# A softmax without maxima, with its sums judged on the chip and a branch to a second version

## Chip, core and metric

One core of one Trainium2 chip runs the whole program. The metric is the device time of one execution in microseconds (us). Before the change three runs took 253.1, 253.52 and 254.39 us, median 253.52 us. The times of the parts below come from one further execution, recorded by the hardware profiler.

## What is computed

Grouped attention feeds a gated layer. There are 8 batches, 16 query heads, 4 key/value heads, 384 positions, head size 64. Cut to what matters:

```python
scores = q @ k.T / 8                       # per batch and head, 384 x 384
scores = scores - scores.max(-1)
attn = exp(scores);  attn = attn / (attn.sum(-1) + 1e-9)
x = (attn @ v)                             # 8 x 384 x 1024 after joining the heads
h = relu(x @ w_in);  u, v = h[:512], h[512:]
v_n = (v - mean(v)) / sqrt(var(v) + 1e-6)
v_s = w_spatial @ v_n + b_spatial          # mixes positions
out = (u * v_s) @ w_out                    # 8 x 384 x 1024, float32
```

The inputs q, k and v are normal draws times 0.1.

## The kernel before

The five engines are TensorE (PE; its weight loads are shown as PEld), VectorE (DVE), ScalarE (ACT), GpSimd (POOL) and SyncE (SP, which only issues DMAs). Each runs its own stream of instructions and waits for the others by semaphores. The order within every stream is the order in which the Python code emits instructions (`manual_schedule`), so a line's place in the code is its place in its engine's queue.

**Attention.** A batch is 18 steps of `scores` (L224): two matmuls give 128 keys by 1024 queries, and ACT takes the exponential (L240) straight from PSUM with a scale and no maximum. `weigh` (L242) multiplies the exponentials with v, to which a column of ones is appended, so that the sum of the exponentials comes out beside the weighted values. DVE then takes the reciprocal of four sums (L257) into a small tile `r` and scales the values with it (L259). There are 96 such calls, 12 for each batch.

**The gated layer.** `stream` (L424) is a generator that emits the gated layer's matmuls one after another: `v_tile` (L288), `u_block` (L358), `gate` (L375), `project` (L395). The main loop (L594) draws from it between the attention's steps, so that PE has matmuls while ACT works on exponentials. Inside `u_block`, at its fourth matmul, `normal` (L311) is emitted: ACT makes the reciprocal deviation, DVE the term `nmr` (L316), and POOL three times a normalised tile `vn` (L322). `gate` multiplies `vn` (L380), DVE adds the bias (L390), and the product with u (L392) goes to POOL, in the last batch alternately to POOL and DVE. `project` multiplies with w_out (L406), copies out of PSUM on DVE or ACT (L415) and lets SP issue the output DMA, in the last batch one for each piece (L419).

**The end.** After the last batch's attention nothing is left but the rest of the generator (L615): the last `v_tile`s, `u_block`s, `gate`s and `project`s. Then the launch code (L641) drains every engine, lets SP wait for the output DMAs, and joins the engines.

Of the kernel before, what the change touches and what calls it, by code (L numbers as in the profile page):

```python
# [17 lines left out]
def kernel(  # L18
# [59 lines left out]
    def load_k(b, eng=nc.sync):  # L78
        eng.dma_start(stage_tile("k", b), rows_of(k[b]))

    def load_v(b, eng=nc.sync):
        eng.dma_start(stage_tile("v", b), rows_of(v[b]))

    def load_q(b, j, eng=nc.sync):
        eng.dma_start(stage_tile("q", b, j), rows_of(q[b, 8 * j : 8 * j + 8]))
# [63 lines left out]
    def cast_k(b, eng, js=(0, 1)):  # L149
        if b not in k16s:  # L150
            k16s[b] = ld.tile([P, 2, NT, 2, D], FP16, name=f"k16_{b}", tag="k16")
        src = stage["k", b].rearrange("p (j h) (t d) -> p j h t d", h=2, t=NT)
        for hh in range(2):
            eng.tensor_copy(
                k16s[b][:, js[0] : js[-1] + 1, :, hh, :], src[:, js[0] : js[-1] + 1, hh]
            )

    def cast_v(b, eng):
        eng.tensor_copy(
            v1[b % 2][:, :, :, 0:D].rearrange("p g t d -> p (g t) d"),  # L160
            stage["v", b].rearrange("p g (t d) -> p (g t) d", t=NT),
        )

    def cast_q(b, j, eng, lo=0, hi=NT, other=None):
        if (b, j) not in q16s:
            q16s[b, j] = ld.tile([P, NT, G, 2, D], FP16, name=f"q16_{b}_{j}", tag="q16", bufs=4)
        src = stage["q", b, j].rearrange("p (h i) (t d) -> p h t i d", h=2, t=NT)
        for hh in range(2):
            f = other if hh and other else eng.tensor_copy
            f(q16s[b, j][:, lo:hi, :, hh, :], src[:, hh, lo:hi])  # L170
# [14 lines left out]
    def k_transposes(b, j, eng):  # L185
        ps = ps_ck.tile([P, S], FP16, name=f"kps_{b}_{j}", tag="ck")
        for t in range(NT):
            nc.tensor.transpose(
                ps[:, t * P : (t + 1) * P],
                k16s[b][:, j, t].rearrange("p h d -> p (h d)"),  # L190
                ident16,
            )
        eng(k_tile(b)[:, j], ps)

    def q_transposes(b, j, t, *engs):
        w = G // len(engs)
        for x, eng in enumerate(engs):
            ps = ps_ck.tile([P, w * P], FP16, name=f"qps_{b}_{j}_{t}_{x}", tag="ck")
            for i in range(w):
                nc.tensor.transpose(  # L200
                    ps[:, i * P : (i + 1) * P],
                    q16s[b, j][:, t, x * w + i].rearrange("p h d -> p (h d)"),
                    ident16,
                )
            eng(q_tile(b, j)[:, t, x * w * P : (x + 1) * w * P], ps)
# [13 lines left out]
        )  # L219


    aTs, avs, x16s, xts = {}, {}, {}, {}

    def scores(n):  # L224
# [17 lines left out]
    def weigh(b, m, hh):  # L242
        qt, j = divmod(m, 2)
        av = ps_av.tile([P, G, D + 1], FP32, name=f"av_{b}_{m}_{hh}", tag="av")
        for i in range(G):
            for t in range(NT):
                nc.tensor.matmul(  # L247
                    av[:, i, :],
                    aTs[b, m][:, t, hh, i * P : (i + 1) * P],
                    v1[b % 2][:, 2 * j + hh, t, 0 : D + 1],  # L250
                    start=(t == 0),
                    stop=(t == NT - 1),
                )
        if m == 0 and hh == 0:
            x16s[b] = att.tile([P, NT, NB, P], FP16, name=f"x16_{b}", tag="x16")
        r = small.tile([P, G, 1], FP32, name=f"r_{b}_{m}_{hh}", tag="r")
        nc.vector.reciprocal(r, av[:, :, D : D + 1])  # L257
        blk = 4 * j + 2 * hh
        nc.vector.tensor_tensor(  # L259
            x16s[b][:, qt, blk : blk + 2].rearrange("p k (i d) -> p (k i) d", i=2),  # L260
            av[:, :, 0:D],
            r.to_broadcast([P, G, D]),
            ALU.mult,
        )
# [13 lines left out]
    def x_turn(b, qt, lo, hi):  # L278
        nc.sync.dma_start(
            x_tile(b)[:, qt, lo:hi],  # L280
            x16s[b][:, qt, lo:hi].rearrange("p k s -> p (k s)"),
            transpose=True,
        )


    mvs, v_rs, v_ns, uTs, gTs, osbs = {}, {}, {}, {}, {}, {}
# [24 lines left out]
    def normal(b):  # L311
        rstd = small.tile([P, NT], FP32, name=f"rstd_{b}", tag="rstd")
        nmr = small.tile([P, NT], FP32, name=f"nmr_{b}", tag="nmr")
        nc.scalar.activation(rstd, mvs[b][:, :, 1], AF.Ln, bias=eps_t)
        nc.scalar.activation(rstd, rstd, AF.Exp, scale=-0.5)
        nc.vector.scalar_tensor_tensor(  # L316
            nmr, mvs[b][:, :, 0], -1.0, rstd, op0=ALU.mult, op1=ALU.mult
        )
        v_ns[b] = []
        for st in range(NT):  # L320
            vn = moe.tile([P, DH], FP16, name=f"vn_{b}_{st}", tag="vn", bufs=6)
            nc.gpsimd.tensor_scalar(  # L322
                vn,
                v_rs[b][st],
                rstd[:, st : st + 1],
                nmr[:, st : st + 1],
                op0=ALU.mult,
                op1=ALU.add,
            )
            v_ns[b].append(vn)  # L330
# [27 lines left out]
    def u_block(b, m):  # L358
        pu = ps_ck.tile([P, 512], FP32, name=f"pu_{b}_{m}", tag="ck")
        for kt in range(NB):  # L360
            nc.tensor.matmul(  # L361
                pu[:, 0:S].rearrange("p (t s) -> p t s", t=NT),
                w_in16[:, kt, m * P : (m + 1) * P],
                x_tile(b)[:, :, kt],
                start=(kt == 0),
                stop=(kt == NB - 1),
            )
            if m == 0 and kt == 3:
                normal(b)
            if kt < NB - 1:  # L370
                yield S
        nc.scalar.activation(uT_tile(b)[:, m, :], pu[:, 0:S], AF.Relu)
        yield S
# [21 lines left out]
    def project(b, tt, half):  # L395
        last = b == B - 1
        rows = out[b].rearrange("(p t) d -> p t d", t=NT)
        if half == 0:
            osbs[b, tt] = ops.tile([P, DM], FP32, name=f"osb_{b}_{tt}", tag="osb")
        osb = osbs[b, tt]  # L400

        cuts = (512, 768, 1024) if last and tt == NT - 1 and half else (512 * half, 512 * half + 512)
        for i, (lo, hi) in enumerate(zip(cuts, cuts[1:])):
            po = ps_ck.tile([P, 512], FP32, name=f"po_{b}_{tt}_{half}_{i}", tag="ck")
            for m in range(NM):
                nc.tensor.matmul(  # L406
                    po[:, 0 : hi - lo],
                    gTs[b][:, m, tt * P : (tt + 1) * P],
                    w_out16[:, m, lo:hi],
                    start=(m == 0),  # L410
                    stop=(m == NM - 1),
                )
                if m < NM - 1:
                    yield hi - lo
            (nc.scalar.copy if half and not i else nc.vector.tensor_copy)(  # L415
                osb[:, lo:hi], po[:, 0 : hi - lo]
            )
            if last:
                nc.sync.dma_start(rows[:, tt, lo:hi], osb[:, lo:hi])  # L419
            elif half:  # L420
                nc.sync.dma_start(rows[:, tt, :], osb)
            yield hi - lo

    def stream():  # L424


        for b in range(B):
            last = b == B - 1
            if b == 0:
                yield from v_tile(0, 0)  # L430
                yield from v_tile(0, 1)
                yield from u_tile(0, 0)
                yield from v_tile(0, 2)
                yield from u_tile(0, 1)
                yield from u_tile(0, 2)
            else:
                yield from v_tile(b, 1)
                yield from v_tile(b, 2)
                for m in range(NM):
                    yield from u_block(b, m)  # L440
                    if last and m == 2:
                        yield from gate(b, 0)
                        yield from gate(b, 1)
            for m in range(2 if last else 0, NM):
                yield from gate(b, m)
            if not last:
                yield from v_tile(b + 1, 0)
            for tt in range(NT):
                for half in range(2):
                    yield from project(b, tt, half)  # L450

    HV = NB * 512
# [161 lines left out]
            run_fill(COLS / NU)  # L614
    for _ in fill:  # L615
        pass
    assert not todo and not turns
# [1 line left out]
_INS = ['q', 'k', 'v', 'moe_w_in', 'moe_w_spatial', 'moe_b_spatial', 'moe_w_out']  # L619
# [26 lines left out]
```

## Time and profile before

| | |
|---|---|
| median of three runs | 253.52 us |
| the profiled execution: its own time | 253.12 us |
| the profiled execution: span from first to last instruction | 251.3 us |
| busy: PE, DVE, ACT, POOL | 240.9, 139.7, 168.2, 98.3 us |
| granted TensorE clock | 1.0 throughout |
| last matmul ends, last copy out of PSUM ends | 247.5, 247.9 us |
| last output DMA issued by SP | 248.3 us |

The span leaves out 1.8 us of the execution's own time. "Busy" adds up what an engine's instructions took; an engine that isn't busy waits for a semaphore. The chain of waits follows the last instruction back to what released it, and so tells which engine's time is also the program's.

### The profile page before, as it was taken

Reading aid. Unit: us, or ns where it says so; the run is one execution under the profiler, and the core shown is the slowest. Engines: PE = TensorE matmul, PEld = TensorE weight load, DVE = VectorE, ACT = ScalarE, POOL = GpSimd, SP = SyncE. Lnnn points to the kernel's source line nnn. Section 1 sums busy time; section 2 is a strip of 40 time slices with the busy share of each in tenths; the row PEclk is TensorE's granted clock in tenths of the full one; section 3 lists DMA queues with packets and bytes.
Section 4 is the critical chain, followed back from the end, with each engine's and each line's share of the span. In section 5 each row is a group of like instructions: output and inputs, shape, how many; then the busy total and the mean of one; then the engine's idle time right before and its main releaser. Section 6 shows DMA issues by size and latency. Waiting matters only on the chain.

```text
span 251.3 us, 6020 instructions
## 1 busy us (share of the span) xinstructions
PE 240.9 (96%) x2430; PEld 125.7 (50%) x2430; DVE 139.7 (56%) x368; ACT 168.2 (67%) x215; POOL 98.3 (39%) x142
## 2 busy tenths in 40 slices
PE   7898998999999999999999999999999999999883
PEld 7564657534455444544455445544455445544442
DVE  2455776854626755474626655474636655465462
ACT  3996566678696687768696687768696687741211
POOL 2698837871035701392036602391035003320320
PEclk9999999999999999999999999999999999999999
DMA  7999998999289964997399956997392452106006
GB/s 179 268 285 251 301 285 238 297 224 265 88 182 330 171 230 85 266 233 216 121 199 324 185 200 66 281 253 227 111 171 49 111 183 44 34 12 250 0 22 232
DMA packets 73981, 46.93 MB, mean 187 GB/s; under 512 B 48113, under 2 KB 68913, under 8 KB 73953
## 3 DMA queue, kind: packets, MB, share of 16 engines
q1 hardware_dynamic: 68832, 37.63, 59.4%
q0 software_dynamic: 4080, 8.65, 13.8%
q8 instruction: 19, 0.31, 0.5%
q10 hardware_dynamic: 1040, 0.26, 0.5%
q14 instruction: 10, 0.07, 0.1%
HBM read 25.95 MB, written 12.58 MB: 153 GB/s over the span
## 4 chain that ended last, share of the span: by engine, by line
PE 87%; DVE 7%; issue 1%; ACT 1%; POOL 1%; POOLq 0%; DVEq 0%
PE av L247 17%; PE pv L294 16%; PE sc L233 15%; PE po L406 15%; PE pu L361 13%; PE psp L380 6%; PE warm L504 3%; DVE stats L306 2%; DVE vr L304 2%; DVE x L259 2%; PE pu L344 1%; PE qps L200 1%; ACT aT L240 1%; POOL vn L322 1%; PE xps L275 1%
## 5 line engine op out<-in xcount | busy, mean ns | idle before, releaser
L240 ACT ACTIVATE aT<-sc 128x1024 f16<-128x1024 f32 x144 | 139.6, 1021 | 52.9 <-PE sc L233 52.7
L247 PEld LDWEIGHTS <-aT 128*128 128x128 f16 x1152 | 43.4, 97 | 32.9 <-DVE x L259 12.9
L322 POOL TENSOR_SCALAR vn<-vr,rstd,nmr 128x512 f16<-128x512 f32 x24 | 18.1, 767 | 99.6 <-DVE r L257 85.7
L247 PE MATMUL av<-v,aT 128*128 128x65 f16 x1152 | 52.3, 194 | 1.6 <-DVE x L259 1.2
L294 PE MATMUL pv<-w_in,xt 128*128 128x512 f16 x192 | 49.5, 378 | 0.0
L257 DVE RECIPROCAL r<-av 128x4 f32<-128x4 f32 x96 | 17.1, 178 | 58.3 <-PE av L247 57.8
L406 PE MATMUL po<-w_out,gT 128*128 128x512 f16 (+1 forms) x196 | 48.2, 375 | 0.9 <-POOL gT L392 0.9
L233 PE MATMUL sc<-qT,kT 64*128 64x512 f16 x288 | 45.0, 382 | 0.7 <-ACT aT L240 0.4
L259 DVE TENSOR_TENSOR x<-av,r 128x256 f16<-128x256 f32 x96 | 40.7, 424 | 3.4
L361 PE MATMUL pu<-xt,w_in 128*128 128x384 f16 x224 | 41.7, 326 | 0.0
L392 POOL TENSOR_TENSOR gT<-g,uT 128x384 f16<-128x384 f32 x30 | 26.5, 914 | 29.4 <-DVE g L390 29.4
L361 PEld LDWEIGHTS <-w_in 128*128 128x128 f16 x224 | 20.2, 97 | 14.7 <-issue 2.5
L406 PEld LDWEIGHTS <-gT 128*128 128x128 f16 x196 | 17.0, 97 | 19.4 <-issue 2.9
L170 POOL CAST q<-q 128x768 f16<-128x768 f32 (+1 forms) x36 | 24.9, 732 | 3.1 <-DMA q<-in_q_dram 3.1
L415 DVE COPY osb<-po 128x512 f32<-128x512 f32 (+1 forms) x25 | 16.8, 671 | 11.6 <-PE po L406 11.6
L294 PEld LDWEIGHTS <-xt 128*128 128x128 f16 x192 | 16.2, 97 | 13.5 <-issue 0.7
L415 ACT COPY osb<-po 128x512 f32<-128x512 f32 (+1 forms) x24 | 13.9, 580 | 12.4 <-PE po L406 12.3
L304 DVE TENSOR_SCALAR vr<-pv 128x512 f32<-128x512 f32 x24 | 16.5, 687 | 10.2 <-PE pv L294 10.0
L233 PEld LDWEIGHTS <-kT 64*128 64x128 f16 x288 | 8.9, 94 | 26.6 <-issue 24.4
L380 PE MATMUL psp<-wsT,vn 128*128 128x384 f16 x96 | 19.6, 326 | 0.6 <-POOL vn L322 0.6
L390 DVE TENSOR_TENSOR g<-psp,bias_b 128x384 f32<-128x384 f32 x32 | 16.4, 552 | 5.9 <-PE psp L380 5.9
L306 DVE BATCH_NORM_STATS2 stats<-vr 128x6 f32<-128x512 f32 x24 | 16.7, 695 | 0.8
(49 smaller groups left out, 125.8 us busy)
## 6 DMA issues: line engine op xcount, KB each, us to landing
out_dram<-osb SPq DMA_DIRECT2D x21, 512.0 KB, 2.9
q<-in_q_dram SPq DMA_DIRECT2D x10, 768.0 KB, 7.2
q<-in_q_dram POOLq DMA_DIRECT2D x4, 768.0 KB, 10.4
v<-in_v_dram SPq DMA_DIRECT2D x6, 384.0 KB, 8.7
w_in<-in_moe_w_in_dram POOLq DMA_DIRECT2D x4, 512.0 KB, 9.7
k<-in_k_dram SPq DMA_DIRECT2D x5, 384.0 KB, 4.2
out_dram<-osb SPq DMA_DIRECT2D x5, 256.0 KB, 2.0
q<-in_q_dram SPq DMA_DIRECT2D x2, 512.0 KB, 7.2
```

The source lines that it names most:

```text
L170: f(q16s[b, j][:, lo:hi, :, hh, :], src[:, hh, lo:hi])
L233: nc.tensor.matmul(sc[:, hh], kTs[b][half, j, t * P : (t + 1) * P], qTs[b, j][half, qt], start=True, stop=True,)
L240: nc.scalar.activation(aTs[b, m][:, t], sc, AF.Exp, scale=scale)
L247: nc.tensor.matmul(av[:, i, :], aTs[b, m][:, t, hh, i * P : (i + 1) * P], v1[b % 2][:, 2 * j + hh, t, 0 : D + 1], start=(t == 0), stop=(t ...
L259: nc.vector.tensor_tensor(x16s[b][:, qt, blk : blk + 2].rearrange("p k (i d) -> p (k i) d", i=2), av[:, :, 0:D], r.to_broadcast([P, G, D]) ...
L294: nc.tensor.matmul(pv, x_tile(b)[:, st, kt], w_in16[:, kt, DH:DFF], start=(kt == 0), stop=(kt == NB - 1),)
L306: nc.vector.bn_stats(stats, vr)
L361: nc.tensor.matmul(pu[:, 0:S].rearrange("p (t s) -> p t s", t=NT), w_in16[:, kt, m * P : (m + 1) * P], x_tile(b)[:, :, kt], start=(kt == 0 ...
L380: nc.tensor.matmul(psp[:, 0:S], v_ns[b][st][:, m * P : (m + 1) * P], wsT16[:, st, :], start=(st == 0), stop=(st == NT - 1),)
L392: by.tensor_tensor(gTs[b][:, m, :], g, uTs[b][:, m, :], ALU.mult)
L406: nc.tensor.matmul(po[:, 0 : hi - lo], gTs[b][:, m, tt * P : (tt + 1) * P], w_out16[:, m, lo:hi], start=(m == 0), stop=(m == NM - 1),)
L415: (nc.scalar.copy if half and not i else nc.vector.tensor_copy)(osb[:, lo:hi], po[:, 0 : hi - lo])
```

## The change

The reciprocals of all 49152 sums are no longer kept in a rotating small tile, but in one tile `r_all` of 128 x 384 float32, each call of `weigh` writing its four columns. In the last batch, right behind `normal`, `judge` lets DVE test every reciprocal (not over 20, not under 2e-5), reduce the result to one value for each partition, and convert it. In the last batch's `project`, ahead of its second row block, `verdict` adds the 128 values by a matmul with a column of ones, and DVE makes an integer flag of it. At the end of the program every engine loads that flag into a register, and where it is set, a branch computes all batches again, with the maximum of each query subtracted. The second computation, `again`, stands in the program in full (8 batches, unrolled).

```diff
+    r_all = cst.tile([P, B * HQ * NT], FP32, name="r_all")
...
-        r = small.tile([P, G, 1], FP32, name=f"r_{b}_{m}_{hh}", tag="r")
+        at_r = (6 * b + m) * 2 * G + hh * G
+        r = r_all[:, at_r : at_r + G].unsqueeze(2)
         nc.vector.reciprocal(r, av[:, :, D : D + 1])
...
+    def judge():
+        shape = [P, B * HQ * NT]
+        big = cst.tile(shape, FP32, name="big_enough")
+        fine = cst.tile(shape, FP32, name="fine")
+        nc.vector.tensor_scalar(big, r_all, 20.0, None, op0=ALU.is_le)
+        nc.vector.scalar_tensor_tensor(fine, r_all, 2e-5, big, op0=ALU.is_ge, op1=ALU.mult)
+        each = cst.tile([P, 1], FP32, name="each")
+        nc.vector.tensor_reduce(each, fine, mybir.AxisListType.X, ALU.min)
+        each16 = cst.tile([P, 1], FP16, name="each16")
+        nc.vector.tensor_copy(each16, each)
+        ones = cst.tile([P, 1], FP16, name="ones")
+        nc.vector.memset(ones, 1.0)
+        judged["each"], judged["ones"] = each16, ones
+
+    def verdict():
+        count = ps_av.tile([1, 1], FP32, name="count", tag="av")
+        nc.tensor.matmul(count, judged["each"], judged["ones"], start=True, stop=True)
+        flag = cst.tile([1, 1], mybir.dt.int32, name="flag")
+        nc.vector.tensor_scalar(flag, count, float(P), None, op0=ALU.is_lt)
+        judged["flag"] = flag
+
+    def attend_with_maximum(b):
+        load_k(b)
+        for j in range(2):
+            load_q(b, j)
+        load_v(b)
...
+        for qt in range(NT):
+            for h in range(HQ):
...
+                nc.vector.tensor_reduce(top, s, mybir.AxisListType.X, ALU.max)
...
+    def again():
+        for d in (xts, uTs, gTs, mvs, v_rs, v_ns, osbs, kTs, qTs, k16s, q16s):
+            d.clear()
+        for b in range(B):
+            attend_with_maximum(b)
...
+            for tt in range(NT):
+                for half in range(2):
+                    for _ in project(b, tt, half):
+                        pass
...
             if m == 0 and kt == 3:
                 normal(b)
+                if b == B - 1 and not judged:
+                    judge()
...
             for tt in range(NT):
                 for half in range(2):
+                    if last and (tt, half) == (1, 0):
+                        verdict()
                     yield from project(b, tt, half)
...
     for _ in fill:
         pass
+
+    with tc.If(nc.values_load(judged["flag"], min_val=0, max_val=1) > 0):
+        again()
```

## The prediction

> **What bounds the kernel now.** I read the page's chain of waits first, then the timeline of the last 17 us, where all that the change adds to the straight path is placed, then the instructions of the launch code's line L641, and last the queues that fetch instructions. From the page:
>
> ```profile
> span 251.3 us, 6020 instructions
> PE 240.9 (96%) x2430; PEld 125.7 (50%) x2430; DVE 139.7 (56%) x368; ACT 168.2 (67%) x215; POOL 98.3 (39%) x142
> ...
> PE 87%; DVE 7%; issue 1%; ACT 1%; POOL 1%; POOLq 0%; DVEq 0%
> ```
>
> The chain runs through PE for 87% of the span, and PE is busy for 96% of it. DVE has 44% idle. So DVE work added early is free; but in the last batch the chain leaves PE, as the timeline from 235 us shows (start, duration, engine, line, operation, in brackets the idle time before and who ended it):
>
> ```profile
> 235.28 0.16 DVE L316 SCALAR_TENSOR_TENSOR nmr<-mv,rstd 128x3 f32<-128x3 f32 x1 [0.60 <-ACT rstd L315]
> 235.64 2.26 POOL L322 TENSOR_SCALAR vn<-vr,rstd,nmr 128x512 f16<-128x512 f32 x3 [13.84 <-PE pu L361]
> ...
> 237.21 0.34 PE L380 MATMUL psp<-wsT,vn 128*128 128x384 f16 x1 [0.22 <-POOL vn L322]
> ...
> 237.96 0.82 PE L380 MATMUL psp<-wsT,vn 128*128 128x384 f16 x4 [0.41 <-POOL vn L322]
> 238.41 1.04 DVE L390 TENSOR_TENSOR g<-psp,bias_b 128x384 f32<-128x384 f32 x2 [2.97 <-PE psp L380]
> ...
> 239.11 0.91 POOL L392 TENSOR_TENSOR gT<-g,uT 128x384 f16<-128x384 f32 x1 [1.21 <-DVE g L390]
> 239.56 0.89 DVE L392 TENSOR_TENSOR gT<-g,uT 128x384 f16<-128x384 f32 x1
> ```
>
> Here PE waits 0.22 and 0.41 us for POOL's three `vn`: whatever delays POOL delays PE, and all that follows. DVE, meanwhile, is idle from 235.44 (`nmr` ends) to 238.41: the "2.97" in its row. That hole is where `judge` falls.
>
> The end, by the instructions of L641 (q marks an engine's sequencer; durations are min/median/max in ns, then first and last start):
>
> ```profile
> L641 SPq EVENT_SEMAPHORE  x11: 17/28/28, 248.7 to 251.3; - x11
> ...
> L641 SPq DRAIN  x3: 7/7/7, 250.5 to 250.8; - x3
> L641 PEldq DRAIN  x2: 13/560/1107, 246.4 to 250.9; - x2
> L641 ACTq DRAIN  x2: 14/208/401, 247.1 to 250.8; - x2
> L641 DVEq DRAIN  x2: 19/240/461, 247.5 to 250.9; - x2
> ```
>
> The sequencers of PE, ACT and DVE have reached the end of the program at 246.4, 247.1 and 247.5 and then idle: SP's drain comes only at 250.5, behind the last output DMAs, whose landing the line's own answer gives:
>
> ```profile
> L419 SPq DMA_DIRECT2D out_dram<-osb x7: 332/332/404, 243.9 to 248.3; - x7
> ...
> DMA to landing us min/median/max: 1.9/2.0/2.1
> ```
>
> 248.3 plus 2.0 is 250.3. From 250.5 the joining takes 0.8 us to 251.3. So PE has 4.1 us, ACT 3.4 and DVE 3.0 us of cover at the end, and SP, last issue over at 248.7, has 1.6.
>
> **The change part by part.**
>
> *The reciprocals' place* (L256): the same 96 reciprocals of 128x4 at 178 ns, written elsewhere; the old tile's rotation was among DVE's own instructions. Nothing either way.
>
> *`judge`* adds five DVE instructions. No row has a plain compare over 384 columns; the nearest are the two-input add at L390 (128x384, 0.552 us) and the casts of 192 columns at L154 (0.34 us). Compare 0.36 to 0.56, combined compare 0.42 to 0.56, reduction 0.56, convert and memset some 0.1 each (the memset at L140 took 0.06): 1.5 to 1.9 us with gaps. From 235.5 that ends by 237.4, a microsecond ahead of DVE's next work: the hole covers it. Without that hole it would cost its 1.9 us.
>
> What the hole doesn't cover is POOL. At 239.56 DVE starts its own product at L392, both inputs in SBUF, while POOL's product runs until 240.02; DVE takes 0.885 us, ending 0.43 us after POOL. The second pair, at 241.83, does the same (0.875 us). L390, as long but with one input in PSUM, takes 0.552. So a DVE instruction with two SBUF inputs waited until POOL's was over. `judge`'s combined compare has two SBUF inputs and comes, at about 236.1, in the middle of `vn`. Either it slips in between the first and the second `vn`, and POOL's remaining two are late by its 0.45 us; or it waits until POOL is done at 237.9, `judge` ends at 239.2, the first `g` is 0.8 us late, and by way of `g` and `gT` some 0.5 us of that reaches PE. Bounds: 0, if POOL isn't held and DVE slips in, and 0.9, if the first compare holds POOL as well. I take **+0.5**, where both orders meet. [...]
>
> *`verdict`* adds one small matmul with its weight load on PE (load rows 97 ns, a 512-column matmul every 0.22 us): 0.03 to 0.2, I take **+0.1**, as PE is without gaps there. DVE's flag falls into one of its 1 us waits for `po` near 244 and is ready before anyone reads it. Queued behind it is only the copy at 244.92, with 1.03 us to spare.
>
> *The branch*. Every engine loads the flag, compares and jumps over `again`, whose `scores`, transposes and projections exceed the main program on PE. The trace shows no register load and no branch. Nearest rows: semaphore instructions of 17 to 51 ns and SP's DMA issues of 0.33 to 0.40 us. Three such steps cost 0.1 to 1.2 us; I take 0.6, nearer to an issue that also reads memory. The jump's target isn't what comes next in the stream, so it may have to be fetched:
>
> ```profile
> q8 instruction: 19, 0.31, 0.5%
> ...
> q14 instruction: 10, 0.07, 0.1%
> ```
>
> 0.31 MB is 64 bytes for each of PE's 4860 loads and matmuls: q8 is PE's instruction stream, in 16 KB packets of 0.5% x 16 x 251.3 / 19 = 1.06 us; q14's packets took about 0.4 us. To that a DMA's way is added, at most the 2.0 us of the output rows, since those carry their data in it. A missed fetch is thus 1.1 to 3.1 us on PE and 0.4 to 2.4 on the others; I take the upper ends, since a fetch starts only at the jump. PE: 246.4 + 0.6 + 3.1 = 250.1. DVE: 247.5 + 0.6 + 2.4 = 250.5. Both just fit under SP's 250.5. SP itself: 248.7 + 0.6 = 249.3, covered if its target has been fetched ahead (its `again` is short, 60 DMAs and their waits), and 251.7 if not: +1.2. Where the paths meet, SP's semaphores for DMAs have to be brought to what the other path would have left, say ten instructions at 0.06 us, the spacing of its rows at L641: 0 to +0.6. Bounds of the tail 0 and +4 (rival 2); with SP's fetch half likely I take **+0.9**. [...]
>
> Sum: 0.5 + 0.1 + 0.9 = +1.5 us. On the profiled execution 253.12 becomes 254.6 (span 252.8); on the median, 0.4 us above it, 253.52 becomes **255.0**. A measurement of this kernel tells about 0.5%, 1.27 us, from no change.
>
> **The rivals.**
>
> 1. *All hidden.* `judge` finds POOL free and the fetches end under the last landing: +0.1 to 0.4, 253.8, no change to be measured. For it: the covers of 3.0 to 4.1 us. Against: DVE's fits only just, and the two L392 rows. It decides if DVE's and SP's ways to the join end before 250.5. Chance 0.27.
> 2. *The branch in series with the outputs.* If engines meet, or SP waits for the landings, before the flag is loaded, load and fetch stand behind 250.5 uncovered: 0.6 + 2.4 to 3.1, with the 0.6 of the other parts about +3.8, 257.3. [...] Against: each engine only needs the flag. Chance 0.17.
> 3. *Faster*, if a new order of instructions ends PE's 0.63 us of waiting for `vn`: 253.0. Nothing is removed from the path, so 0.04.
> 4. *The branch is taken*: a second computation, at least +250 us. With scores near 0 each sum is about 384, its reciprocal 0.0026, far inside 2e-5 to 20, and 8 x 48 columns fill the tile: 0.01.
>
> **How the numbers follow.** My forecast has 0.51, its own range 253.9 to 256.3; about 0.08 of that lies under 1.27 us. Slower by over 0.5%: 0.43 + 0.17 + 0.01 = 0.61. Within 0.5%: 0.27 + 0.08 = 0.35. Faster: 0.04. The range, 253.4 to 257.8, takes in most of rivals 1 and 2.
>
> **What would show it.** In the changed kernel's timeline: DVE's five new instructions between 235 and 239, the combined compare beside `vn`, and either a gap of 0.4 to 0.6 us between POOL's `vn`, or DVE's compare of over 1 us; the waits of PE for `vn` grown from 0.63. At the end: instruction packets on q8 and q14 behind 246, the engines' register loads, and SP's drain against the last landing. I am wrong if `vn` still takes 2.26 us and `g` starts as early as before; if the last landing still precedes the end by 1.0 us only; or if engines wait for each other ahead of the branch.

## The result and the profile after

The changed kernel takes 257.22 us, median of four runs (256.67 to 257.57), against 253.31 us for the kernel before on the same chip: a ratio of 1.0137 [1.0101, 1.0174], +3.9 us by the medians and +3.5 by the ratio. The ratios here and below leave out two runs, of 259.28 and 260.13 us, that lie over 1.5% above the fastest of their kernel. Its profiled execution took 257.57 us, with a span 4.45 us longer than before's. From its page, the span, the busy line and the chain of waits:

```profile
span 255.8 us, 6055 instructions
...
PE 241.8 (95%) x2431; PEld 125.6 (49%) x2431; DVE 141.5 (55%) x374; ACT 168.2 (66%) x215; POOL 98.6 (39%) x142
...
PE 82%; DVE 7%; DMA 4%; POOL 2%; issue 1%; ACT 1%; POOLq 0%; DVEq 0%
```

The busy times have grown by 1.8 us on DVE and by about one on PE; a second computation would have shown here. PE's share of the chain falls from 87 to 82%, and "DMA 4%" is new. That isn't the end of the program: in the view of the chain by time the DMA pieces lie at the start (k, from 0.74 to 4.1 us) and at 50.5 to 56.7 us (q), and its last piece is still DVE's last copy. What the sequencers do behind that copy the chain doesn't follow.

**Where the 4.45 us lie.** Matching each matmul of after with the same one of before gives the lateness along the program. It is 0.88 us by 60 us, constant until 235 us, 1.26 behind the first gates, 1.46 behind `verdict`, and the rest comes after the last matmul:

| stretch | before | after | us |
|---|---|---|---|
| loads and transfers until 60 us | | | +0.88 |
| `vn` beside `judge` | 2.26 | 2.64 | +0.38 |
| `verdict` in PE's queue | | | +0.20 |
| SP's last output issue (L419, now L529) | 0.40 | 2.26 | +1.86 |
| end of that issue to the last output packet | 1.12 | 1.29 | +0.17 |
| last output packet to the end | 1.56 | 2.52 | +0.96 |

The first row isn't the change. The kernel with a branch over one instruction, below, has the same instructions up to the branch, and at the same place it is 0.05 us early; over all the kernels below that place lies between 0.11 early and 0.86 late. What the change costs in this trace is 3.57 us.

The stretch of `judge` (timeline: start, duration, engine, line, operation, in brackets the idle time before and who ended it):

```profile
236.16 0.16 DVE L424 SCALAR_TENSOR_TENSOR nmr<-mv,rstd 128x3 f32<-128x3 f32 x1 [0.60 <-ACT rstd L423]
236.24 0.35 DVE L295 TENSOR_SCALAR big_enough<-r_all 128x384 f32<-128x384 f32 x1
236.53 2.64 POOL L430 TENSOR_SCALAR vn<-vr,rstd,nmr 128x512 f16<-128x512 f32 x3 [13.85 <-PE pu L469]
236.63 0.56 DVE L296 SCALAR_TENSOR_TENSOR fine<-r_all,big_enough 128x384 f32<-128x384 f32 x1
...
238.47 0.34 PE L490 MATMUL psp<-wsT,vn 128*128 128x384 f16 x1 [0.41 <-POOL vn L430]
...
239.66 1.05 DVE L500 TENSOR_TENSOR g<-psp,bias_b 128x384 f32<-128x384 f32 x2 [1.69 <-PE psp L490]
...
245.20 0.08 PEld L308 LDWEIGHTS <-each 128*1 128x1 f16 x1 [0.42 <-issue]
```

The combined compare (L296) isn't slowed: 0.56 us. POOL is: the first of its three `vn` took 1.14 us and the others 0.76, and the row grows from 2.26 to 2.64. That is so although the `vn`'s recorded start lies 0.10 us ahead of the combined compare's. The last row is `verdict`'s weight load, with 0.42 us of idle time on the loader ahead of it where the matmuls came back to back before.

At the end, the instructions of the branch's line L731 (q is an engine's sequencer; durations min/median/max in ns, then first and last start), and SP's of the launch code's line L757:

```profile
L731 SPq EVENT_SEMAPHORE  x8: 17/17/17, 253.5 to 254.1; - x8
...
L731 PEldq TENSOR_LOAD <-flag x1: 768/768/768, 247.9 to 247.9; - x1
...
L731 PEldq COMPARE_BRANCH  x1: 4178/4178/4178, 248.8 to 248.8; - x1
...
L731 SPq TENSOR_LOAD <-flag x1: 527/527/527, 252.0 to 252.0; - x1
...
L731 PEldq EVENT_SEMAPHORE  x1: 51/51/51, 253.1 to 253.1; - x1
```

```profile
L757 SPq EVENT_SEMAPHORE  x14: 17/28/28, 254.2 to 255.7; - x14
...
L757 SPq DRAIN  x3: 7/7/13, 254.9 to 255.2; - x3
```

PE loads the flag at 247.9, ahead of the array's end at 248.9, and then stands at its branch for 4.2 us. The queue q8, PE's instruction stream, has two packets more than before (21 for 19) and q14 five more (15 for 10). But PE is through at 253.1, and DVE and ACT sooner: SP's drain at 254.9 still ends the program, as before. SP is late because of this row, the output DMAs:

```profile
L529 SPq DMA_DIRECT2D out_dram<-osb x7: 332/332/2260, 245.2 to 249.7; - x7
...
DMA to landing us min/median/max: 2.0/2.1/4.3
```

The last issue takes 2.26 us where the longest took 0.40 before. In the trace it runs from 249.72 to 251.98, and PE's fetch of its branch target, one packet of 16 KB on q8, from 249.80 to 251.53. Only then does SP load the flag (252.0). The two outputs before it suffer too: their issues were over at 249.2 and 249.6, yet they land at 253.1 and 253.4, 4.3 and 4.1 us after the issues began, where none took more than 2.1 before. The last one lands at 253.7. SP's own jump costs 0.5 us from the branch to the next instruction, and there follow 20 semaphore instructions until the drain, from 253.46 to 254.83, most of them 0.06 to 0.07 us apart: eight at the join and twelve waits. Before, the drain came 0.37 us after the last output's wait had been met (250.14 to 250.51); now it comes 1.16 us after it (253.74 to 254.90).

### The profile page after: what moved, and what is told of

It is laid out like the page before. It is cut to its first block, busy times and chain, and to the rows that moved or that the text cites. A ratio compares the mean times of both kernels' runs of the same rounds, so it can differ in the third digit from the quotient of the medians.

```text
span 255.8 us, 6055 instructions
## 1 busy us (share of the span) xinstructions
PE 241.8 (95%) x2431; PEld 125.6 (49%) x2431; DVE 141.5 (55%) x374; ACT 168.2 (66%) x215; POOL 98.6 (39%) x142
## 4 chain that ended last, share of the span: by engine, by line
PE 82%; DVE 7%; DMA 4%; POOL 2%; issue 1%; ACT 1%; POOLq 0%; DVEq 0%
PE av L248 16%; PE pv L402 15%; PE sc L234 14%; PE po L516 14%; PE pu L469 13%; PE psp L490 5%; DMA qT<-q 2%; DVE x L261 2%; PE warm L616 1%; DVE stats L414 1%; POOL gT L502 1%; DVE vr L412 1%; DMA k<-in_k_dram 1%; PE pu L452 1%; PE qps L200 1%
## 5 line engine op out<-in xcount | busy, mean ns | idle before, releaser
L259 DVE RECIPROCAL r_all<-av 128x4 f32<-128x4 f32 x96 | 17.2, 179 | 58.5 <-PE av L248 58.0
L261 DVE TENSOR_TENSOR x<-av,r_all 128x256 f16<-128x256 f32 x96 | 40.8, 425 | 3.4
```

The lines of the kernel that those rows point to most:

```text
L261: nc.vector.tensor_tensor(x16s[b][:, qt, blk : blk + 2].rearrange("p k (i d) -> p (k i) d", i=2), av[:, :, 0:D], r.to_broadcast([P, G, D]) ...
```

## The experiments

For the end of the program the theory is that PE's fetch of its branch target holds SP's last output issue, and that the join's semaphores add the rest; the rival is that the engines' own late return from the branch (PE at 253.1) sets the end. For `judge` the theory is that a DVE instruction with two inputs in SBUF and a POOL instruction running at the same time lengthen one another, as the first `vn` (1.14 us) beside the combined compare suggests; the rival, that the first compare (0.35 us), with one input, lengthens it. Gains and losses below are against runs of the kernel before on the same chip.

### Without the branch

```diff
-    with tc.If(nc.values_load(judged["flag"], min_val=0, max_val=1) > 0):
-        again()
```

This kernel computes the flag and doesn't use it.

> The changed kernel without the branch: judge, verdict and flag stay, nobody loads the flag, and the second computation is not in the program. Theory A (judge and verdict cost 0.4 + 0.2 us by POOL's held vn and PE's pause; the rest of the 3.9 us is the branch): 253.9 us, +0.6 on the kernel before; vn still 2.6 us; last SP issue 0.4 us long; end of the span as far behind the last landing as before. Theory B (the 0.9 us by which the changed kernel was late already at 57 us of its span belongs to the change): +1.5 us, 254.8. Theory C (the branch is free, judge costs it all): over 256.5.

Measured: 254.04 us, ratio 1.0012 [0.9998, 1.0027]. In its trace `vn` takes 2.64 us and PE pauses for `verdict`, together 0.58 us late, and the last issue takes 0.40. So the branch holds most of the 3.9 us: what is left without it is 0.3 us by the ratio, which its interval doesn't tell from nothing, 0.55 by the medians and 0.58 by the trace.

### The branch alone

The flag is set to 0 at the start; no reciprocal is tested.

```diff
+    flag = cst.tile([1, 1], mybir.dt.int32, name="flag")
+    nc.vector.memset(flag, 0)
+    judged["flag"] = flag
...
-                if b == B - 1 and not judged:
-                    judge()
...
-                    if last and (tt, half) == (1, 0):
-                        verdict()
```

> The changed kernel without judge and verdict: the flag is a constant 0, set at the start, so the test of the sums is left out; the branch over the second computation is as in the change. Theory A: +2.8 to 3.3 us, 256.1 to 256.6; vn back at 2.26 us; SP's last DMA issue stretched to 2 us or more beside PE's instruction fetch; PE's branch over 4 us, DVE's and ACT's stalls near 3.1 us. Theory C: within 0.5 us of the kernel before.

Measured: 256.57 us, 1.0098 [1.0065, 1.0131], 2.5 us by the ratio. `vn` is back at 0.77 us each, and the matmuls are no later from 235 us on. The last issue takes 2.26 us, beside a q8 fetch from 249.02 to 250.84:

```profile
L530 SPq DMA_DIRECT2D out_dram<-osb x7: 332/333/2257, 244.6 to 249.0; - x7
```

With the 0.3 us above that is 2.8 of the change's 3.5 us by the ratio; the difference lies within the intervals.

### A branch over one instruction

The branch stays, with all loads and compares, over a body of one instruction. The second computation is left out.

```diff
-        again()
+        nc.gpsimd.memset(b32, 0.0)
```

> The changed kernel with a branch whose body is one memset in place of the second computation, which is left out: flag, register loads, compare and jump stay, but the target is the next few instructions. Theory A (the far target is what costs): no fetch at the end, SP's last issue 0.4 us, branches over in 0.5 us; +0.9 to 1.4 us on the kernel before, 254.2 to 254.7. Rival D (loading the flag, comparing and joining cost the same whatever the body): 256.5 to 257.2, like the change.

Measured: 254.17 us, 1.0026 [1.001, 1.0042], 0.7 us by the ratio, of which 0.58 are `judge` and `verdict`. q8 has 19 packets, as before. From branch to next instruction the engines need 0.17 to 0.28 us, the last issue 0.40:

```profile
L529 SPq DMA_DIRECT2D out_dram<-osb x7: 332/333/397, 244.3 to 248.8; - x7
```

A branch with a near target is thus almost free here: the register loads of 0.54 to 0.76 us and the jump lie under the outputs, and from the last packet to the end it is 1.72 us where before had 1.56. This body issues no DMA, and the eight semaphore instructions that SP runs at the join in the change are not there.

### Far for PE alone

```diff
-        again()
+        w2 = ps_ck.tile([P, 512], FP32, name="w2", tag="ck")
+        for _ in range(1500):
+            nc.tensor.matmul(w2[:, 0:P], ident16, ident16, start=True, stop=True)
```

The body is long for PE alone; for the other engines there is nothing to skip. It leaves the second computation out.

> The changed kernel with a branch body of 1500 matmuls on PE alone in place of the second computation, which is left out: only PE's target is far. Theory A (PE's 16 KB fetch blocks SP's last DMA issue, and PE's own stall of 4 us ends the program): SP's last issue again about 2 us, PE's branch about 4 us, +3.0 to 3.5 us, 256.3 to 256.8. Rival E (the issue is held by the fetches of ACT and DVE, or by nothing of the kind): SP's last issue 0.4 us; then PE's stall alone sets the end, +2.2 to 2.8 us, 255.5 to 256.1.

Measured: 256.09 us, 1.0085 [1.0054, 1.0116]. Its output DMAs:

```profile
L529 SPq DMA_DIRECT2D out_dram<-osb x7: 332/332/2241, 244.9 to 249.5; - x7
...
DMA to landing us min/median/max: 2.0/2.1/4.3
```

PE's jump alone brings the long issue back (249.48 to 251.72, fetch 249.53 to 251.35), and PE itself is away for 4.3 us, until 252.85. DVE and ACT go on after 0.2 us. The time, 256.09, falls under the range of theory A and just into that of rival E, so it decides nothing; the trace does. The issue is long, and SP's waits at the end pass one after the other except for the last output's, which lands at 253.50, after PE is back. Here too the eight semaphore instructions are missing: from the last packet to the end it is 1.71 us.

### Far for DVE and ACT alone

```diff
-        again()
+        z = cst.tile([P, 8], FP32, name="z")
+        z2 = cst.tile([P, 8], FP32, name="z2")
+        for _ in range(2000):
+            nc.vector.memset(z, 0.0)
+        for _ in range(700):
+            nc.scalar.copy(z2, z)
```

> The changed kernel with a branch body of 2000 memsets on DVE and 700 copies on ACT in place of the second computation, which is left out: only DVE's and ACT's targets are far. [...] Rival (all fetches hold SP alike): last issue 1 us or more.

Measured, in one run: 255.34 us (before 253.54). The output DMAs:

```profile
L529 SPq DMA_DIRECT2D out_dram<-osb x7: 332/332/403, 244.5 to 249.1; - x7
...
DMA to landing us min/median/max: 2.0/2.1/2.7
```

DVE stalls for 3.2 us and ACT for 2.6, yet the issue keeps its 0.40. So stalls as such don't make the long issue. Whether an 8 KB fetch could hold an issue isn't shown, as these two (on q14, at 249.74 and 250.23) start when the last issue is over, at 249.47. They go with a late landing instead: from the end of the last issue to the last packet it takes 1.88 us instead of 1.12. And in this kernel the rival has a part: one of SP's last waits stands 0.2 us for DVE, which is back from its branch only at 252.2, after the last landing (251.8).

### Two inputs in SBUF, met by POOL the other way round

Meant to shift the two-input compare by 0.2 us to behind the start of `vn`.

```diff
-        nc.vector.tensor_scalar(big, r_all, 20.0, None, op0=ALU.is_le)
-        nc.vector.scalar_tensor_tensor(fine, r_all, 2e-5, big, op0=ALU.is_ge, op1=ALU.mult)
+        nc.vector.tensor_reduce(big[:, 0:1], r_all, mybir.AxisListType.X, ALU.max)
+        nc.vector.scalar_tensor_tensor(fine, r_all, 2e-5, r_all, op0=ALU.is_ge, op1=ALU.mult)
```

> The change with its first compare replaced by a reduction, so that of the two instructions beside POOL's first vn only the combined compare remains, with two SBUF inputs (both r_all; the upper bound is judged by the reduction and not used further, so the test is weaker here). Theory F (the two-input compare holds POOL): a vn is 1.1 us again, wherever the compare falls, or the compare itself takes over 1 us because POOL holds it; PE waits some 0.4 us longer for vn than before. [...]

The time misses what was meant: multiplied by `r_all` in place of a truth value, the tested values are about 0.0026 and not 1, their sum stays under 128, and the branch is taken. The run took 1825.42 us, so the second computation costs about 1572 us. What stands ahead of the branch can be read all the same:

```profile
235.80 0.55 DVE L295 TENSOR_REDUCE big_enough<-r_all 128x1 f32<-128x384 f32 x1
...
236.09 2.57 POOL L430 TENSOR_SCALAR vn<-vr,rstd,nmr 128x512 f16<-128x512 f32 x3 [13.84 <-PE pu L469]
236.26 1.00 DVE L296 SCALAR_TENSOR_TENSOR fine<-r_all 128x384 f32<-128x384 f32 x1
```

The reduction, one input, overlaps the first `vn` by 0.26 us and neither is slowed (0.55 and 0.77 us). The compare, two inputs, starts 0.17 us into the first `vn` and takes 1.00 us instead of 0.56, ending 0.40 us after that `vn`; POOL's second `vn`, which starts under the compare, takes 1.07 instead of 0.77. So either engine's instruction can be the one that takes longer, and the reduction's overlap speaks against the rival for one input as such. What decides between them the recorded starts don't tell: a `vn` that starts 0.17 us ahead of the compare keeps its 0.77 us here, and one that starts 0.10 us ahead of it in the change takes 1.14. Whether the change's first compare, with one input, lengthens a `vn` can't be read off here: this kernel has no such compare, and in the change it overlaps `vn` by 0.06 us only.

### Judged earlier

`judge` with two reductions and tests of one column, ahead of the last batch's second `v_tile`; `verdict` where PE waits for `vn` anyway. The branch is unchanged.

```diff
-        nc.vector.tensor_scalar(big, r_all, 20.0, None, op0=ALU.is_le)
-        nc.vector.scalar_tensor_tensor(fine, r_all, 2e-5, big, op0=ALU.is_ge, op1=ALU.mult)
+        nc.vector.tensor_reduce(top, r_all, mybir.AxisListType.X, ALU.max)
+        nc.vector.tensor_reduce(low, r_all, mybir.AxisListType.X, ALU.min)
...
+            if b == B - 1 and m == 0 and st == 1 and "flag" not in judged:
+                verdict()
...
+                if last:
+                    judge()
```

> The change with judge made of two reductions and three operations on single columns, emitted ahead of the last batch's v tiles, where DVE waits 2 us for PE and POOL is idle; verdict's matmul stands in PE's wait for the second vn. The branch is unchanged. Theory A: vn back at 2.26 us, no 0.2 us pause of PE before the second row block, so 0.6 us less than the change, 256.3 to 256.7. Rival (judge's cost only moves: the last projection of the batch before gets its copies late): 257.0 or more.

Measured: 256.41 us, 1.0106 [1.0083, 1.0128], 2.7 us by the ratio. The three `vn` take 0.77 us each and PE is no later behind `verdict` than ahead of `judge`: both terms are 0. The branch's part is all there, with a last issue of 2.48 us. That the flag was ready 3.7 us earlier (POOL's load at 241.9 instead of 245.6) helps no one, as PE comes to its branch only behind its own matmuls, at 247.7.

### Telling the engines of the jump

The edits mark the branch, for named engines, as likely taken, and each of them then has a hint instruction (45 to 51 ns in the first kernel's trace). In the traces these instructions run at the head of the program, at 0.7 to 0.8 us, and not where the edits mark them, so what follows is the effect of a hint given at the start. First on after itself, then on the kernel that judges early:

```diff
+                        tc.mark_branch_hint_location("again", "LikelyTaken", (E.PE,))
...
+                        tc.mark_branch_hint_location("again", "LikelyTaken", (E.DVE, E.Activation))
...
-    with tc.If(nc.values_load(judged["flag"], min_val=0, max_val=1) > 0):
+    with tc.If(nc.values_load(judged["flag"], min_val=0, max_val=1) > 0, label="again"):
```

> The change with a prefetch hint for the branch on PE (ahead of the last projection), DVE and ACT (ahead of its second row block), nothing else. Theory A (the stall is the fetch of the target, and the fetch also holds SP's last DMA issue): packets on q8 and q14 near 242 to 246 in place of 249 to 251, branches over in 0.5 us, SP's last issue 0.4 us, the time as with the tiny body plus 0.5 us of semaphores: 254.3 to 255.0. Rival (the jump empties the stream and refetches whatever was held): unchanged at 257; or the fetch now holds the earlier output issues and part of the 2 us stays: 255.5 to 256.5.

> Both of the last two: early judge by reductions, verdict in PE's wait, hints for PE, DVE and ACT. Theory A: 253.8 to 254.4, the kernel before plus 0.3 to 0.9 us of flag loads, jump and semaphores behind SP's last issue. Rival as in each of the two.

Measured: 257.81 us, 1.0163 [1.0141, 1.0184], and 256.24 us, 1.0107 [1.0088, 1.0126]. No gain: the first is no faster than after, the second no faster than the same kernel without hints. From the first, PE's hint, its branch, and the output DMAs (L530 here):

```profile
L762 PEldq BRANCH_PREFETCH_HINT  x1: 50/50/50, 0.8 to 0.8; - x1
```

```profile
L736 PEldq COMPARE_BRANCH  x1: 393/393/393, 249.1 to 249.1; - x1
```

```profile
L530 SPq DMA_DIRECT2D out_dram<-osb x7: 332/332/405, 245.5 to 250.1; - x7
...
DMA to landing us min/median/max: 2.0/2.3/4.4
```

The stalls are gone (PE 0.45 us instead of 4.3, DVE 0.62, ACT 0.48), and so is the long issue. This kernel settles the rival for PE: PE is at the join at 249.6, and the program ends no sooner. For once PE has jumped, one more packet of 16 KB comes on q8 from 250.33 to 251.95 (what it carries isn't shown), and now the issued outputs are late beside that: their last packet lands 3.20 us after the issue's end instead of 1.12, and SP waits 2.06 us from its branch to the next instruction, a semaphore at the join that waits for the landing. In the early kernel the fetch comes at 248.83, and the last packet 2.85 us after the issue. The trade is nearly even: what the issue gains, the landing loses. The first kernel's trace loses another 0.38 us near 242 us, where DVE starts a `g` 0.43 us after the semaphore that it waited for (0.07 in after); the rows don't show why, and the early kernel doesn't have it.

### The branch in the middle

If fetches must not stand beside the last outputs, the jump has to come earlier. Here the flag is ready before the last batch's first `gate`; the branch is put there, the rest of the last batch is its likely side and lies last in the program, and `again` is its other side. The first version has hints for all five engines, the second for PE, DVE and ACT, the third none.

```diff
+                        yield "branch"
...
+    tc.mark_branch_hint_location("again", "LikelyTaken", (E.PE, E.DVE, E.Activation))
+    with tc.If(
+        nc.values_load(judged["flag"], min_val=0, max_val=1) < 1,
+        preferred_fallthrough_block=False,
+        label="again",
+    ) as cmp:
+        for _ in fill:
+            pass
+    with cmp.Else():
+        again()
```

> The early judge by reductions, with the branch moved: flag, loads and jump come ahead of the last batch's first gate, where PE waits for POOL's vn, and the rest of the last batch is the branch's other side, which lies last in the program, so that at its end nobody jumps. A prefetch hint for all five engines. Complete: both versions are in the program. Theory A (a far jump costs by its fetches, and these cost only where SP issues or lands outputs): fetches near 235 to 239, no packets on q8 and q14 behind 246, SP's last issue 0.4 us, last landing 1.9 us behind it; what stays is 0.8 us of added semaphores on SP: 254.0 to 254.6. Rival (PE's load and jump stand in its way in the middle as they do at the end): PE pauses 1 us or more ahead of the first gate, 255.0 to 256.0.

> [...] The moved branch with five hints had executions at 253.5 and others up to 259.3. If the spread comes from hints for POOL or SP: all executions at 253.5 to 254.3. If it comes from where the fetches of PE, ACT and DVE fall among the waits for vn: the spread stays, median 254.3 to 255.

> The moved branch without any hint. Theory A: PE's branch takes 4 us or more ahead of the first gate, of which 0.6 us lie in its wait for vn and some 1 us in the matmuls queued ahead: +2.5 to 3.5 us, 256 to 257. If executions with hints that take 257 are those in which a hint came to nothing, this kernel takes 257 always. Rival (the fetch hides in the middle): 254 to 254.6.

| hints for | median of runs | from, to | ratio to before | PE's branch | last issue |
|---|---|---|---|---|---|
| five engines | 254.63 of 12 | 253.53, 259.28 | 1.0055 [1.002, 1.0089] | 0.39 | 0.34 |
| PE, DVE, ACT | 253.41 of 12 | 252.98, 256.63 | 0.9992 [0.9965, 1.0018] | 0.39 | 0.33 |
| none | 257.09 of 4 | 255.61, 260.13 | 1.012 [1.0065, 1.0175] | 3.38 | 0.34 |

The version with three hints does all that the change does, at no cost that can be measured. Its output DMAs:

```profile
L528 SPq DMA_DIRECT2D out_dram<-osb x7: 332/332/345, 243.8 to 248.3; - x7
...
DMA to landing us min/median/max: 1.7/2.0/2.0
```

They are as before, from the first start (243.8, before 243.9) to the landing. PE loads the flag and branches between 235.45 and 236.44, while matmuls handed on earlier still run (until 236.95), and its matmuls are 0.07 us early at the end. Without hints the same place costs PE 2.1 us: its lateness goes from 0.38 to 2.49 there. That is read from the fastest of the four runs without hints; the slower ones have no trace. No kernel here beats the kernel before.

Why the version with five hints scatters isn't settled. In its profiled execution (253.58 us, span 251.8) nothing is slow, and the slow ones have no trace. It differs from the second in the hints for POOL and SP alone; three of its twelve runs lie near 257 us and one at 259.28, of the second's one lies at 256.63. The mean granted clock is 0.987 to 0.993 in these five and 0.998 to 1.0 in the others; whether the lower clock is a cause of the delay or a consequence isn't shown.

## Why the prediction was right or wrong

The direction was right and the measured time lies in the range, but 257.2 is 2.2 us over the 255.0, and outside the forecast's own 253.9 to 256.3. That the wide range, 253.4 to 257.8, holds it is luck: its upper part was there for the branch in series with the outputs, a mechanism that didn't come.

- **The reciprocals' place**, 0: right. Nothing changes between 60 and 235 us.
- **`judge`**, +0.5: 0.38, and where the prediction put it: `vn` grew beside the combined compare, from 2.26 to 2.64 us. Neither of the two orders that the prediction gave came as drawn. The compare fell on the first `vn` and took 0.56 us, and that `vn` ran long, 1.14 us, so that there is no gap between the `vn`; the sign set for it was wrong in that. Which of the two runs long doesn't follow from the order of the recorded starts, since that `vn` starts 0.10 us ahead of the compare. The first compare is still running then and overlaps the `vn` by 0.06 us; whether it has a part isn't shown.
- **`verdict`**, +0.1: 0.20, the upper end.
- **The branch**, +0.9: about 3.0, and this is the term that was mis-sized. Its parts:
  - *The steps ahead of the jump*, 0.6: on PE from load to branch 0.87 us, on the others 0.6 to 0.9. Near in size.
  - *The fetch*, at most 3.1 on PE and 2.4 on the others: 4.3, 3.2 and 3.1. The way of an output DMA was the wrong measure. On PE the fetch's packet starts 1.05 us after the branch does, takes 1.73, and PE goes on 1.5 us after it is in: a second wait that no output row showed.
  - *The cover*: the prediction let PE's way to the join compete with SP's 250.5. It came at 253.1 and still wasn't last, since beside the same fetch SP's last issue had grown by 1.86 us and the last three outputs landed at 253.1 to 253.7. This coupling is what the sum left out: it treated the fetches as time of the engine that jumps and the outputs as time of SP, with nothing between them.
  - *SP's own target*: its jump took 0.5 us, and no packet on q14 ended in that time, so it waited for no fetch that the trace shows, as hoped.
  - *The semaphores at the join*, 0 to +0.6: all that follows the last packet grew by 0.96 us, with eight instructions more at the join and twelve waits in place of nine. Without the eight, in the kernels with a body of one instruction or of PE's alone, it grew by 0.16 and 0.15 only.

**The rivals.** "All hidden" is out by the interval, and so are "faster" and "the branch is taken". "The branch in series with the outputs" gave 257.3, almost the measured number, but not for its reason: SP loads the flag 1.2 us ahead of the last packet, and no engine meets another first. That something at the end stands in series was true; it was the last outputs behind one fetch, not the branch behind the landings.

How far a branch jumps counts in these kernels: from branch to next instruction PE, DVE and ACT took 3.1 to 4.3 us for the far target of the change, 0.17 to 0.28 for the near one of a body of one instruction.

## What to carry to other kernels

A branch that is never taken still costs a jump over its body, and a far jump without a hint cost PE, DVE and ACT 2.6 to 4.5 us each at the end of these kernels; what it cost the program here was decided by where the fetch fell. Put it where work already handed on covers it and no output is on its way, with the likely side last in the program and PE, DVE and ACT told of it (253.41 us here, against 257.22 for the change); a hint for a branch at the very end only moved the collision from the issue (0.41 us again) to the landing (2.85 and 3.20 us behind it). When a change adds transfers of any kind, instructions among them, ask which other transfers they meet before adding up times by engine.

## What was not expected of the hardware

- **An instruction fetch can hold another engine's DMA issue.** In four kernels whose PE fetched a far target (after, the branch alone, PE's body alone, judged earlier) SP's last issue took 2.24 to 2.48 us and ended 0.37 to 0.45 us after the fetch, which is an issue's usual length. Where PE fetched nothing then, it took 0.33 to 0.40. The moment matters: in the four the fetch starts 0.01 to 0.08 us after the issue does; in the two kernels with hints and the branch at the end it starts 0.26 and 0.31 us after it, and the issue keeps its 0.41. Why, no trace shows.
- **Output packets already issued came later beside a fetch**: 1.12 us from the issue's end to the last packet before, 1.88 beside 8 KB fetches, 3.20 beside one of 16 KB.
- **Overlapping, POOL's and DVE's instructions took longer, in both directions**: the first `vn` 1.14 us instead of 0.77 beside the change's combined compare, the compare 1.00 instead of 0.56 where it starts deeper inside a `vn`.
- **The clock falls in the second computation**: with the branch taken, the page's row of granted clock goes from 9 tenths to between 5 and 7, and its mean over the span is 0.621.
